# Vectors spread by TensorE and a reordered first batch in an attention and MLP kernel

## The chip, the cores and the metric

One core of a Trainium2 chip. The metric is device microseconds of one execution; a kernel is run several times, and medians are quoted with the lowest and highest run. The profile is one more execution, taken by the hardware profiler, whose span is 1 to 2 us shorter than the timed runs.

## The reference

```python
# q: 8 x 16 x 384 x 64, k and v: 8 x 4 x 384 x 64 (four q heads share a k/v head), all float32
x   = softmax(q @ k.T / 8) @ v          # heads side by side: 8 x 384 x 1024
a1  = alpha1 * x + beta1
tok = einsum('ts,bsd->btd', w_tok, a1)  # the token mix, w_tok 384 x 384
u   = x + lam * tok
a2  = alpha2 * u + beta2
ch  = relu(a2 @ w_ch1) @ w_ch2          # W1 1024 x 4096, W2 4096 x 1024
out = u + lam * ch
```

`alpha1`, `beta1`, `alpha2`, `beta2` and `lam` are vectors of 1024.

## The kernel before

The kernel works through eight batches. A batch has a *side* part (attention, token mix, transposes of `a2`) and a *main* part (`h` = a2 @ W1, `ch` = h @ W2). While TensorE does the main part of one batch, units of the next batch's side part are dropped between its matmuls. Only the side part of the first batch has nothing to hide behind: that is the **prologue**, which ends at the first `h` matmul. I call "main stage" the stretch from there to the first `h` matmul of the second batch.

What the vectors are for: on chip the kernel needs alpha1·lam (`g1`), beta1·lam (`h1`), `lam` and `alpha2` (`al2`) repeated on all 128 partitions, and gets them by broadcast loads, each of which reads the same row of HBM once for every partition (512 KB a vector, as 128 + 384 KB or in one load on the page):

```python
    def bcast(eng, t, ap, lo, hi):
        src = bass.AP(tensor=ap.tensor, offset=ap.offset + lo, ap=[[0, P], [1, hi - lo]])
        eng.dma_start(out=t[:, lo:hi], in_=src)
    # ... cut ...
            t = sb.tile([P, NST, P], f32, tag="tmp", name="a1f", bufs=4)
            nc.vector.tensor_tensor(out=t, in0=x[:, :, cols(p)], in1=bc(g1, p), op=MUL)
            a1s[p] = sb.tile([P, NST, P], bf, tag="a1", name="a1", bufs=2)
            eng = nc.gpsimd if first and p < NP - 2 else nc.vector
            eng.tensor_tensor(out=a1s[p], in0=t, in1=bc(h1, p), op=ADD)
    # ... cut: the prologue's loads ...
        load_k(0)
        nc.scalar.dma_start(out=qst, in_=q[0, :G]...)     # q of heads 0 to 3
        load_q(0, [0], G)                                 # q of heads 4 to 15, GpSimd, casts to bf16
        make_identity(nc, ident)
        load_q(0, [1, 2], G)
        nc.sync.dma_start(out=vst, in_=v[0]...)
        nc.gpsimd.tensor_copy(out=vt[0][:, :, :, :D], in_=vst...)
        place_k(0, 0)
        # ... cut ...
        load_k(1)
        for t, ap in ((g1, moe_alpha1), (lam_t, moe_lam), (h1, moe_beta1)):
            bcast(nc.scalar, t, ap, 0, 256)
            bcast(nc.sync, t, ap, 256, DM)
        bcast(nc.sync, al2, moe_alpha2, 0, DM)
        # ... cut: w_tok, then five tiles of W1; W2 and batch 1's q and v during the units of side(0)
```

A column block `p` is two heads, 128 columns of x. The 18 EXPs of a batch are its softmax tiles. In the prologue the transposes of `a2` of blocks 0 to 4 are DMA transposes, and those of blocks 5 to 7 go through TensorE. In the changed kernel the first batch keeps much of its scratch in `hT`, which nothing else needs yet; so `hT` in its views can be EXP's output, the vector rows, `a` or `a2`.

The softmax here doesn't subtract the row's maximum and nothing guards it: scores larger than these inputs give would overflow.

Of the kernel before, what the change touches and what calls it, by code (L numbers as in the profile page):

```python
# [12 lines left out]
def kernel(  # L13
# [56 lines left out]
    g1, h1, lam_t, al2 = (const.tile([P, DM], f32, tag=n, name=n) for n in ("g1", "h1", "lam", "al2"))  # L70
# [12 lines left out]
    def load_k(b):  # L83
        ks[b] = []
        for h in range(0, Hkv, 2):
            t = sb.tile([P, 2, NST, D], f32, tag="kst", name="kst", bufs=2)
            nc.sync.dma_start(out=t, in_=k[b, h:h + 2].rearrange("h (p st) d -> p h st d", st=NST))
            ks[b].append(t)

    def place_k(b, i):  # L90
        if i == 0:
            k2s[b] = sb.tile([P, NST, Hkv, 2, D], bf, tag="k2", name="k2", bufs=1)
        copies = (nc.vector.tensor_copy, nc.vector.tensor_copy if i else nc.scalar.copy) if b < 2 else [nc.gpsimd.tensor_copy] * 2
        for a in range(2):
            copies[a](out=k2s[b][:, :, 2 * i:2 * i + 2, a, :], in_=ks[b][i].rearrange("p h st d -> p st h d"))
# [5 lines left out]
    def load_q(b, sts=range(NST), i=0):  # L101
        if b not in qrs:
            qrs[b] = sb.tile([P, NST, Hq, D], bf, tag="q_raw", name="q_raw", bufs=1)
        for st in sts:
            nc.gpsimd.dma_start(out=qrs[b][:, st, i:], in_=by_st(q[b])[:, st, i:])
# [8 lines left out]

    def bcast(eng, t, ap, lo, hi):
        src = bass.AP(tensor=ap.tensor, offset=ap.offset + lo, ap=[[0, P], [1, hi - lo]])
        eng.dma_start(out=t[:, lo:hi], in_=src)
# [16 lines left out]
    def tp_ps(shape):  # L134
        return psum.tile(shape, bf, tag="tp", name="tp", bufs=1)
# [6 lines left out]
    def side(b):  # L142
        vb = vt[b % 2]
        x = sb.tile([P, NST, DM], f32, tag="x", name="x", bufs=2)
        xs[b] = x
# [11 lines left out]
        def k_transpose(h0):  # L157
            k2 = k2s[b]
            ps = tp_ps([P, 2 * NST, P])
            for i in range(2 * NST):  # L160
                src = k2[:, i % NST, h0 + i // NST].rearrange("p a d -> p (a d)")
                nc.tensor.matmul(out=ps[:, i, :], lhsT=src, rhs=ident, is_transpose=True,
                                 start=(i == 0), stop=(i == 2 * NST - 1), skip_group_check=True)
            nc.vector.tensor_copy(out=kT[:, :, h0:h0 + 2, :].rearrange("p st h s -> p h st s"),
                                  in_=ps.rearrange("p (h st) s -> p h st s", h=2))

        def q_transpose(g):
            ps = tp_ps([P, 2 * NST, P])
            for i in range(2 * NST):
                h = g * G + 2 * (i // NST)  # L170
                nc.tensor.matmul(out=ps[:, i, :],  # L171
                                 lhsT=qrs[b][:, i % NST, h:h + 2, :].rearrange("p h d -> p (h d)"),
                                 rhs=ident, is_transpose=True, start=(i == 0),
                                 stop=(i == 2 * NST - 1), skip_group_check=True)
            nc.vector.tensor_copy(out=qT[:, :, 2 * g:2 * g + 2, :].rearrange("p st a s -> p a st s"),  # L175
                                  in_=ps.rearrange("p (a st) s -> p a st s", a=2))
# [3 lines left out]
        def scores(i, later=False):  # L180
# [11 lines left out]
            def exp():  # L192
                e = sb.tile([P, 2, 4, P], bf, tag="es", name="es", bufs=EB)
                nc.scalar.activation(out=e, in_=sc, func=EXP, scale=scale_qk)  # L194
                ess[i] = e
# [10 lines left out]
        def av_piece(p, hh):  # L206
# [12 lines left out]
            if hh == 0:  # L219
                if first and p in (0, 2):  # L220
                    r = slice(0, 256) if p == 0 else slice(256, DM)
                    nc.vector.tensor_tensor(out=g1[:, r], in0=g1[:, r], in1=lam_t[:, r], op=MUL)
                    nc.vector.tensor_tensor(out=h1[:, r], in0=h1[:, r], in1=lam_t[:, r], op=MUL)
                return
            rinv = sb.tile([P, 2, NST, 1], f32, tag="rinv", name="rinv", bufs=1)
            nc.vector.reciprocal(out=rinv, in_=av[:, :, :, D:])  # L226
            for hh in range(2):
                c0 = (2 * p + hh) * D
                nc.vector.tensor_tensor(out=x[:, :, c0:c0 + D], in0=av[:, hh, :, :D],  # L229
                                        in1=rinv[:, hh].to_broadcast([P, NST, D]), op=MUL)  # L230
            t = sb.tile([P, NST, P], f32, tag="tmp", name="a1f", bufs=4)
            nc.vector.tensor_tensor(out=t, in0=x[:, :, cols(p)], in1=bc(g1, p), op=MUL)  # L232
            a1s[p] = sb.tile([P, NST, P], bf, tag="a1", name="a1", bufs=2)
            eng = nc.gpsimd if first and p < NP - 2 else nc.vector
            eng.tensor_tensor(out=a1s[p], in0=t, in1=bc(h1, p), op=ADD)  # L235

        def tok(p):
            ps = psum.tile([P, NST, P], f32, tag="av" if first else "sc", name="tok",
                           bufs=1 if first else 2)
            for tt in range(NST):  # L240
                for st in range(NST):
                    nc.tensor.matmul(out=ps[:, tt, :], lhsT=wtokT[:, st, tt * P:(tt + 1) * P],  # L242
                                     rhs=a1s[p][:, st, :], start=(st == 0), stop=(st == NST - 1))
            u = x[:, :, cols(p)]
            nc.vector.tensor_tensor(out=u, in0=ps, in1=u, op=ADD)  # L245
            a2s[p] = sb.tile([P, NST, P], bf, tag="a2", name="a2", bufs=3)
# [15 lines left out]
        def wtok_transpose():  # L262
            wv = wtok_in.rearrange("p tt (s st) -> p tt st s", st=NST)
            for st in range(NST):
                ps = tp_ps([P, NST, P])
                for tt in range(NST):
                    nc.tensor.matmul(out=ps[:, tt, :], lhsT=wv[:, tt, st, :], rhs=ident,
                                     is_transpose=True, start=(tt == 0),
                                     stop=(tt == NST - 1), skip_group_check=True)
                nc.vector.tensor_copy(out=wtokT[:, st, :], in_=ps.rearrange("p a b -> p (a b)"))  # L270
# [10 lines left out]
        if not first:  # L281
            if pe_flip:
# [3 lines left out]
                add(q_transpose, 1)  # L286
            for j in range(NP + 4):
# [3 lines left out]
                if j <= NP:  # L291
                    add(scores2, j)
                    if pe_flip and j in (1, 3):
                        add(q_transpose, 2 + j // 2)
# [8 lines left out]
        add(q_transpose, 0)  # L303
        for i in range(18):
            add(scores, i)
            if i == 1:
                add(q_transpose, 1)
            if i in (5, 9):
                add(q_transpose, i // 4 + 1)
            if i == 4:  # L310
                add(k_transpose, 2)
            if i == 6:
                add(wtok_transpose)
            for p in range(NP):
# [4 lines left out]
                if i == last + 2 and p > 1:  # L319
                    add(tok_flip, p - 2)  # L320
        add(tok, NP - 3)
        add(av_piece, NP - 1, 0)
        add(av_piece, NP - 1, 1)
        add(tok, NP - 2)
        add(a2_transpose, NP - 3)
        add(tok, NP - 1)
        add(a2_transpose, NP - 2)
        add(a2_transpose, NP - 1)
        return us
# [51 lines left out]
    with tc.manual_schedule(engines=order):  # L381

        nc.vector.memset(wtokT, 0.0)
        warm = psum.tile([P, 512], f32, tag="mm", name="warm", bufs=2)
        for _ in range(9):
            nc.tensor.matmul(out=warm[:, :S], lhsT=wtokT[:, 0, :P], rhs=wtokT[:, 1, :],
                             start=True, stop=True)
        load_k(0)
        stage = sb.tile([P, NST, DM], f32, tag="x", name="stage", bufs=2)
        qst = stage[:, 0, :G * NST * D].rearrange("p (h st d) -> p h st d", h=G, st=NST)  # L390
        nc.scalar.dma_start(out=qst, in_=q[0, :G].rearrange("h (p st) d -> p h st d", st=NST))
        load_q(0, [0], G)
        make_identity(nc, ident)
        for t in vt:
            nc.vector.memset(t[:, :, :, D:], 1.0)
        load_q(0, [1, 2], G)
        vst = stage[:, 2, :Hkv * NST * D].rearrange("p (h st d) -> p h st d", h=Hkv, st=NST)
        nc.sync.dma_start(out=vst, in_=v[0].rearrange("h (p st) d -> p h st d", st=NST))
        nc.gpsimd.tensor_copy(out=vt[0][:, :, :, :D], in_=vst.rearrange("p h st d -> p st h d"))
# [3 lines left out]
        load_k(1)  # L403
        for t, ap in ((g1, moe_alpha1), (lam_t, moe_lam), (h1, moe_beta1)):
            bcast(nc.scalar, t, ap, 0, 256)
            bcast(nc.sync, t, ap, 256, DM)
        bcast(nc.sync, al2, moe_alpha2, 0, DM)
        wtok_in = stage[:, 1, :NST * S // 2].bitcast(bf).rearrange("p (tt s) -> p tt s", tt=NST)
        nc.gpsimd.dma_start(out=wtok_in, in_=moe_w_tok.rearrange("(p tt) s -> p tt s", tt=NST))
        be2 = stage[:, 0, DM - NDT:]  # L410
        with nc.allow_non_contiguous_dma(reason="one small vector, once"):
            nc.sync.dma_start(out=be2, in_=moe_beta2.rearrange("(dt di) -> di dt", di=P))
        for c in range(RING):
            load_w1(c)
        loads = {7: [(load_w2, 0, 0, 2)], 25: [(load_q, 1, [0]), (load_q, 1, [1])],
                 31: [(load_q, 1, [2]), (load_v, 1, [0])], 37: [(load_v, 1, [1])], 43: [(load_v, 1, [2])]}
        for i, f in enumerate(side(0)):
# [3 lines left out]
            if i == 4:  # L421
                place_k(0, 1)
# [61 lines left out]
```

## Time and profile before

| | before |
|---|---|
| time, median of 4 (lowest to highest) | 829.96 us (829.51 to 830.88) |
| span of the profile | 828.8 us |
| prologue: start to first `h` matmul | 52.04 us |
| main stage of batch 0: to batch 1's first `h` matmul at 156.08 | 104.04 us |
| the rest | 672.7 us |

The windows view (columns: the stretch; its length, then busy us of PE, PEld, DVE, ACT, POOL, each with its count; the granted TensorE clock; DMA share; GB/s):

```profile
0.00:52.04 52.04, 29.91 (x352) 19.93 (x353) 31.49 (x73) 21.09 (x23) 22.37 (x29) 0.74 1.49 201
52.04:156.08 104.04, 103.02 (x792) 57.75 (x798) 49.72 (x123) 30.80 (x44) 34.30 (x43) 0.98 1.31 183
```

In the prologue no engine is busy for more than 31.5 of 52 us: it is a chain of waits. In the main stage PE is busy for 103.0 of 104.0 us.

### The profile page before, as it was taken

How to read it: one execution, taken by the hardware profiler on the slowest of the kernel's cores; microseconds unless marked ns; L12 is line 12 of the kernel's file. 1: busy time of each engine (PE TensorE's matmuls, PEld its weight loads, DVE VectorE, ACT ScalarE, POOL GpSimd, SP SyncE). 2: the span in 40 equal slices, each digit the busy share in tenths (PEclk: the TensorE clock that was granted, in tenths of full speed). 3: DMA queues.
4: the chain of work that ended last, by engine and by line, in shares of the span. 5: the costliest groups of instructions: out<-in, count | busy, mean ns of one | idle time of the engine just before them, and what ended most of it. 6: DMA issues, size and time to landing. Idle time of an engine off the chain costs nothing.

```text
span 828.8 us, 13904 instructions
## 1 busy us (share of the span) xinstructions
PE 797.1 (96%) x5958; PEld 445.9 (54%) x6011; DVE 350.9 (42%) x728; ACT 219.0 (26%) x287; POOL 187.6 (23%) x229
## 2 busy tenths in 40 slices
PE   5679999999999999999999999999999999999997
PEld 2456555566455654556555664556545565556543
DVE  3854645234452445434443344434444344442222
ACT  3514331233103321043211332133310342102100
POOL 5414441033302250022400224012410221003000
PEclk7869999999999999999999999999999999999999
DMA  9999999799948999499917999379995999119701
GB/s 193 230 145 181 200 210 190 138 175 151 140 97 134 176 169 90 97 166 173 169 46 138 181 169 138 82 128 179 174 91 111 130 176 141 37 55 182 97 38 39
DMA packets 265342, 115.09 MB, mean 139 GB/s; under 512 B 113728, under 2 KB 258496, under 8 KB 265280
## 3 DMA queue, kind: packets, MB, share of 16 engines
q0 software_dynamic: 200832, 83.28, 91.2%
q1 hardware_dynamic: 63488, 30.13, 15.6%
q10 hardware_dynamic: 960, 0.79, 0.4%
q8 instruction: 47, 0.77, 0.4%
q14 instruction: 15, 0.12, 0.0%
HBM read 172.56 MB, written 12.58 MB: 223 GB/s over the span
## 4 chain that ended last, share of the span: by engine, by line
PE 92%; DMA 3%; DVE 2%; issue 1%; ACT 1%; POOL 0%; SPq 0%; DVEq 0%; POOLq 0%
PE h L344 41%; PE ch L368 40%; PE av L217 4%; PE sc L188 4%; PE tok L242 4%; DMA q_raw<-in_q_dram 1%; DMA h<-in_moe_beta_dram 1%; DMA a2T<-a 1%; DVE a L247 1%; ACT hT L352 0%; DVE x L229 0%; DVE x L245 0%; DVE a1f L232 0%; PE tp L171 0%; PE tp L257 0%
## 5 line engine op out<-in xcount | busy, mean ns | idle before, releaser
L344 PE MATMUL h<-a2T,w 128*128 128x384 bf16 (+1 forms) x2048 | 356.6, 327 | 1.2 <-DVE bias L350 0.2
L368 PE MATMUL ch<-w,hT 128*128 128x512 bf16 x1483 | 345.1, 379 | 3.5 <-issue 1.1
L344 PEld LDWEIGHTS <-w 128*128 128x128 bf16 x2048 | 192.9, 98 | 129.4 <-issue 10.6
L127 POOL DMA_DIRECT2D w<-in_moe_w_ch_dram x128 | 112.3, 879 | 549.3 <-PE h L344 514.3
L368 PEld LDWEIGHTS <-hT 128*128 128x128 bf16 x1536 | 142.6, 98 | 155.6 <-issue 4.4
L194 ACT ACTIVATE es<-sc 128x1024 bf16<-128x1024 f32 x144 | 141.2, 1021 | 302.9 <-PE sc L188 302.9
L354 DVE TENSOR_SCALAR hT<-h,bias 128x384 bf16<-128x384 f32 x128 | 78.9, 617 | 186.1 <-PE h L344 185.5
L352 ACT ACTIVATE hT<-h,bias 128x384 bf16<-128x384 f32 x128 | 74.3, 581 | 229.6 <-PE h L344 202.6
L373 DVE TENSOR_TENSOR o<-ch,lam 128x512 f32<-128x512 f32 x48 | 33.0, 688 | 96.9 <-PE ch L368 96.9
L245 DVE TENSOR_TENSOR x<-tok,x 128x384 f32<-128x384 f32 x64 | 35.5, 555 | 82.9 <-PE tok L242 82.9
L217 PEld LDWEIGHTS <-es 128*128 128x128 bf16 x1152 | 52.4, 99 | 23.1 <-issue 1.6
L217 PE MATMUL av<-v,es 128*128 128x65 bf16 x1152 | 56.8, 196 | 0.8 <-ACT es L194 0.6
L242 PE MATMUL tok<-a,wtokT 128*128 128x128 bf16 x576 | 45.0, 226 | 8.8 <-DVE x L245 8.7
L242 PEld LDWEIGHTS <-wtokT 128*128 128x128 bf16 x576 | 38.9, 101 | 22.8 <-issue 6.5
L188 PE MATMUL sc<-qT,kT 64*128 64x384 bf16 (+2 forms) x576 | 46.5, 278 | 0.7 <-DVE qT L175 0.7
L229 DVE TENSOR_TENSOR x<-av,rinv 128x192 f32<-128x192 f32 x128 | 39.8, 352 | 2.3
L247 DVE TENSOR_TENSOR a<-x,al 128x384 bf16<-128x384 f32 x64 | 38.2, 597 | 3.2 <-DMA a2T<-a 1.0
L226 DVE RECIPROCAL rinv<-av 128x6 f32<-128x6 f32 x64 | 12.3, 192 | 59.5 <-PE av L217 59.3
L232 DVE TENSOR_TENSOR a1f<-x,g 128x384 f32<-128x384 f32 x64 | 36.0, 563 | 2.4
L188 PEld LDWEIGHTS <-kT 64*128 64x128 bf16 x576 | 20.1, 95 | 28.0 <-issue 23.6
L374 DVE TENSOR_TENSOR o<-o,x 128x512 f32<-128x512 f32 x48 | 33.2, 692 | 1.6
L235 DVE TENSOR_TENSOR a<-a1f,h 128x384 bf16<-128x384 f32 x58 | 32.5, 561 | 2.2
(38 smaller groups left out, 127.9 us busy)
## 6 DMA issues: line engine op xcount, KB each, us to landing
w<-in_moe_w_ch_dram POOLq DMA_DIRECT2D x135, 512.0 KB, 7.6
out_dram<-o SPq DMA_DIRECT2D x48, 256.0 KB, 2.2
q_raw<-in_q_dram POOLq DMA_DIRECT2D x21, 256.0 KB, 8.8
kst<-in_k_dram SPq DMA_DIRECT2D x16, 192.0 KB, 2.8
w<-in_moe_w_ch_dram POOLq DMA_DIRECT2D x10, 256.0 KB, 12.1
w<-in_moe_w_ch_dram POOLq DMA_DIRECT2D x1, 2048.0 KB, 35.0
v<-in_v_dram POOLq DMA_DIRECT2D x21, 64.0 KB, 8.8
a2T<-a SPq DMA_TRANSPOSE x53, 3.3
```

Source lines behind the costliest of these rows:

```text
L127: nc.gpsimd.dma_start(out=t, in_=w1src[:, :, c * CW * P:(c + 1) * CW * P])
L188: nc.tensor.matmul(out=sc[:, hh, k % 4:k % 4 + n], lhsT=kT[r, sk, 2 * p // G, :], rhs=qT[r, st:st + n, p, :], start=True, stop=True)
L194: nc.scalar.activation(out=e, in_=sc, func=EXP, scale=scale_qk)
L217: nc.tensor.matmul(out=av[:, hh, sq, :], lhsT=ess[k // 4][:, hh, k % 4, :], rhs=vb[:, sk, hk, :], start=(sk == 0), stop=(sk == NST - 1))
L229: nc.vector.tensor_tensor(out=x[:, :, c0:c0 + D], in0=av[:, hh, :, :D], in1=rinv[:, hh].to_broadcast([P, NST, D]), op=MUL)
L232: nc.vector.tensor_tensor(out=t, in0=x[:, :, cols(p)], in1=bc(g1, p), op=MUL)
L242: nc.tensor.matmul(out=ps[:, tt, :], lhsT=wtokT[:, st, tt * P:(tt + 1) * P], rhs=a1s[p][:, st, :], start=(st == 0), stop=(st == NST - 1))
L247: nc.vector.tensor_tensor(out=a2s[p], in0=u, in1=bc(al2, p), op=MUL)
L344: nc.tensor.matmul(out=ps[:, :n], lhsT=w1[:, dt, j * P:(j + 1) * P], rhs=a2T[:, dt, :n], start=(dt == 0), stop=(dt == NDT - 1))
L352: nc.scalar.activation(out=hT[:, nt, :], in_=ps[:, :S], func=RELU, bias=c1)
L354: nc.vector.tensor_scalar(out=hT[:, nt, :], in0=ps[:, :S], scalar1=c1, scalar2=0.0, op0=ADD, op1=mybir.AluOpType.max)
L368: nc.tensor.matmul(out=ps, lhsT=hT[:, nt, ms * P:(ms + 1) * P], rhs=w2[:, nt, cs], start=(nt == 0), stop=(nt == NNT - 1))
```

## The change

The intent is to shorten the prologue. Each vector comes as a few short rows instead of 512 KB. VectorE splits each row into three bf16 parts whose sum is the float32 value, and TensorE spreads them over 128 partitions with a matmul against a selector of ones and zeros (`spread`). In the first batch beta1·lam is no longer added on VectorE or GpSimd: the token mix gets one more matmul, of the row sums of w_tok (`R`) with the beta rows (`H`), zero-padded to 128 rows. q of batch 0 comes by groups of four heads in its own layout and is rearranged by GpSimd. W1's loads are issued after the first of these GpSimd copies and before the others. `a2` has five slots in place of three, and the end of the prologue has a new order, with the split of `lam` (for the main stage) before the small copy that the first `h` matmul waits for.

The diff, cut to its core:

```diff
+            if first:     # first batch: only the multiply is left
+                nc.vector.tensor_tensor(out=a1s[p], in0=x[:, :, cols(p)], in1=bc(g1, p), op=MUL)
+                return
...
-            eng = nc.gpsimd if first and p < NP - 2 else nc.vector
-            eng.tensor_tensor(out=a1s[p], in0=t, in1=bc(h1, p), op=ADD)
+            nc.vector.tensor_tensor(out=a1s[p], in0=t, in1=bc(h1, p), op=ADD)
... token mix
+                if first:
+                    nc.tensor.matmul(out=ps[:, tt, :], lhsT=R[:, tt * P:(tt + 1) * P],
+                                     rhs=H[:, cols(p)], start=False, stop=True)
...
+        def spread(ps_, vs, tag, eng="ACT"):
+            n = len(ps_)
+            ps = psum.tile([P, 4, P], f32, tag=tag, name="vec", bufs=1)
+            w = vs[1] - vs[0]
+            for i, p in enumerate(ps_):
+                nc.tensor.matmul(out=ps[:, i * w:(i + 1) * w], lhsT=sel[:, p:p + 1].to_broadcast([P, P]),
+                                 rhs=rows_b[:, vs[0] * P:vs[1] * P], start=True, stop=True)
+            evac(eng)(out=vecs[:, vs[0]:vs[1], ...], in_=ps[:, :n * w]...)
... units of batch 1's side part
+            for p in range(0, NP if b == 1 else 0, 2):
+                add(spread, (p, p + 1), (2, 4), "tp")
... end of the prologue
         add(a2_transpose, NP - 2)
         add(a2_transpose, NP - 1)
+        add(split, 3, 4)
... loads of the prologue
-        load_k(0)
+        load_k(0, [0])
+        for i, ap in enumerate((moe_alpha1, moe_alpha2, moe_beta1, moe_lam)):
+            nc.sync.dma_start(out=rows_f[:, i * P:(i + 1) * P],
+                              in_=bass.AP(tensor=ap.tensor, offset=ap.offset, ap=[[0, 3], [P, NP], [1, P]]))
+        nc.sync.dma_start(out=vst, in_=v[0].rearrange("h (p st) d -> p h st d", st=NST))
+        load_k(0, [2])
+        load_q4(1)
         make_identity(nc, ident)
+        nc.gpsimd.dma_start(out=wtok_in, in_=moe_w_tok.rearrange("(p tt) s -> p tt s", tt=NST))
+        load_q4(2)
+        load_q4(3)
...
+        nc.gpsimd.tensor_copy(out=vt[0][:, :, :, :D], in_=vst.rearrange("p h st d -> p st h d"))
+        place_q4(1, nc.gpsimd)
+        for c in range(RING - 1):
             load_w1(c)
+        place_q4(2, nc.gpsimd)
-        loads = {7: [(load_w2, 0, 0, 2)], 25: [(load_q, 1, [0]), (load_q, 1, [1])],
-                 31: [(load_q, 1, [2]), (load_v, 1, [0])], 37: [(load_v, 1, [1])], 43: [(load_v, 1, [2])]}
+        loads = {9: [(load_w1, RING - 1), (load_w2, 0, 0, 2)], 20: [(late_loads,)], 30: [(load_q, 1)], 37: [(load_v, 1)]}
```

## The prediction

> **What bounds the kernel now.** I read the page's slices first, then the chain of waits in order of time, then the timelines of VectorE and GpSimd. The slices say where a change can act at all:
>
> ```profile
> span 828.8 us, 13904 instructions
> PE   5679999999999999999999999999999999999997
> ...
> PEclk7869999999999999999999999999999999999999
> ```
>
> From the third slice of 20.7 us on, TensorE is full at full clock: only TensorE work taken away would shorten that, and the change takes none away there. The change lies in the first batch's attention and token mix, a prologue which no matrix work of another batch covers. Its end is the first `h` matmul, at 52.04 us. The busy sums of that stretch (windows view, 0 to 52.04) are PE 29.91, DVE 31.49, ACT 21.09, POOL 22.37 us: no engine is a bound by itself, so waits are. The chain of waits names them (start, length, what):
>
> ```profile
> 3.98 10.29 DMA q_raw<-in_q_dram
> ...
> 17.61 9.60 DMA h<-in_moe_beta_dram
> ...
> 30.05 1.09 DVE a L247
> ...
> 36.45 1.39 DVE a L247
> 37.84 0.03 DVE rinv L226
> 37.87 8.32 DMA a2T<-a
> ...
> 46.28 0.56 DVE a L247
> ...
> 51.74 0.50 PE tp L257 x3
> 52.24 5.56 PE h L344 x24
> ```
>
> Four things. The q of heads 4 to 15 came late, at 14.27. The broadcast vectors came late: g1 and h1 were not complete until 28.2, and all of VectorE's token-mix work stood behind them. From 29 to 42 VectorE ran without a pause, with its `a` multiply at twice its length. Then a slot of `a` had to wait for a DMA transpose. GpSimd's timeline has what lay beside those long multiplies:
>
> ```profile
> 29.72 1.00 POOL L235 TENSOR_TENSOR a<-a1f,h 128x384 bf16<-128x384 f32 x1 [6.80 <-DVE a1f L232]
> 33.12 0.99 POOL L235 TENSOR_TENSOR a<-a1f,h 128x384 bf16<-128x384 f32 x1 [2.40 <-PE av L217]
> ```
>
> And TensorE's clock is half in much of the prologue (0.50 in the 2 us windows from 8 to 16, 32 to 38 and 42 to 54), so the 24 `h` matmuls above take 5.56 us where the same count later in the chain takes 3.92 to 4.03.
>
> [...]
> 1. [...] `a<-x,al` takes 1.07 to 1.39 us beside GpSimd's add and 0.56 us alone (46.28).
> 2. [...] the idle time from 26.8 to 30.07 is followed by windows at 0.50.
> 3. [...] from 5.5 us on, with q's pieces in the queue, the DMA rate falls from about 360 to 160 GB/s, and w1 with longer pieces runs at about 200.
>
> **The change, part by part.** The work on the time is the walk below: I go through the new instruction order of each engine with the durations of the old trace. Durations used: EXP 0.96 apart; a set of scores 0.33 on TensorE when warm (0.54 cold), an `av` pair 0.65 (1.1), a token mix 0.61 (1.1), six transposes 0.35; VectorE per column block: reciprocal 0.22, two multiplies 0.65, g1 multiply 0.48, token-mix add 0.59, al2 multiply 0.47, all start to start and without GpSimd beside it (from 46.28 to 51.13), so 2.4 us; the 768-wide PSUM copy 0.56 on VectorE, and on ScalarE an estimated 0.80 (from its 384-wide copy at 0.48 and EXP's slope of 0.84 ns an element).
>
> Removed: four broadcasts of 512 KB (2 MB at the 300 GB/s seen at 20 to 27 us is 7 us of all DMA engines); the g1 and h1 multiplies by lam (2.75 us of VectorE); GpSimd's six adds and VectorE's two (with them the contention, about 0.5 us on each of four multiplies); the slot wait of 8.3 us, since `a` has five slots in place of three.
>
> Added: the vectors as 24 short rows, two multiplies and five operations to split them, about 2.9 us of VectorE; `spread`, two 256-column matmuls (0.3) and a ScalarE copy of 512 columns (0.57, same slope), four times in the prologue and four in batch 0's main stage; three more matmuls of 128 columns in each token mix (0.61 becomes 0.82); the row sums (about 1 us of VectorE, once); three q and k copies moved from VectorE to ScalarE.
>
> Moved: q comes in 768-byte pieces, each group of heads its own transfer, then a GpSimd copy; W1 is issued after the first such copy; the last W1 tile and W2 later.
>
> The walk. *Start:* k lands as before, 4.05. Scores need only half of q's first group, so the first EXP starts at 6.65 (was 7.59). EXPs 0 to 3 fit without a wait, to 10.5. The split ends at 9.55, the spread at 9.9. q's second group: I estimate landing at 7 [...], the GpSimd copies of v and q end at 9.3 to 9.8, transposes 10.45, VectorE copy 11.1, so EXP 4 starts at 11.55, against 15.5 for EXP 2 before. *Middle:* the weights of the token mix and the row sums hold VectorE to 14.9, scores 6 stand behind them on TensorE, EXP 6 starts at 14.85. From there ScalarE has 12 EXPs, three spread copies (0.57) and three q/k copies (0.80), 15.6 us: with about 1 us of waits EXP 17 ends at 31.4. VectorE has seven `av` groups (1.35) and eight token mixes (1.06), 17.9 us, with about 2 us of waits for TensorE up to 27. *End:* `av` 7 is done at 32.1; VectorE is behind by then: reciprocal of the last pair at 32.8, its g1 multiply to 34.25, the mixes of blocks 6 and 7 follow one after the other through one PSUM buffer (add to 34.75, mix to 35.6, add to 36.2, multiply to 36.8). The transposes of block 7 end 1 us later, but the moved tail puts the split of lam (five operations, 1.25 us) ahead of the small copy which the first `h` matmul waits for: it starts at 38.3.
>
> So the prologue is 52.0 - 38.3 = 13.7 us shorter. Against it: eight spread matmuls in the full main stage, 8 x 0.13 = +1.0. If the clock is warm at the hand-over, the first 24 `h` matmuls save 5.56 - 3.95 = 1.6; I count half, -0.8. 829.9 - 13.7 + 1.0 - 0.8 = 816.4. My walk leaves out small latencies and GpSimd's copies beside VectorE from 12.7 to 15.3; I add 0.6: **817.0 us**.
>
> **The rivals.**
> (a) *TensorE goes cold.* For: it was cold some 27 of the first 54 us, and padding and spreads add to it. Per block, cold: 2.25 x 0.54 + 1.1 + 1.44 + 0.5 = 4.3 us, more than ScalarE's 2.8 and VectorE's 2.4, so it would be the bound. Against: [...] seven dummy matmuls stand in the early gap. I give it 2 to 5 us: 819 to 822.
> (b) *A transfer takes the place of the removed one.* The 2 KB copies of the beta rows are issued at about 9.6 and the first mix needs them at 15; before, a vector of 128 KB took 6.5 to 7.5 us to land. And the DMA transposes took 7.2 to 8.3 us: block 4's, issued at about 30.5, would land at 38.5, just as `h` starts. 0 to 3 us: up to 820.
> (c) *VectorE and ScalarE wait less than I walked*, as the padding and the spread rows end every wait on a vector. The floor is ScalarE: 18 EXPs, four spreads and three copies, 22 us from 6.65, then about 5.5 us for the tail, so `h` at 34: 812 to 813.
> (d) *All hidden*: the main stage then waits for W1, for q of batch 1 or for W2, which is issued later, and the gain is given back. Against: W1's first four tiles should land by about 21 (2 MB at 200 GB/s from 9.5), and batch 1's q at about 42, some 5 us before its transposes are due. 825 and more; I give it 1 in 20.
>
> **Range and chances.** Walk 816.4, (c) to 812.5, (a) and (b) to 822: the range is **812.5 to 822.5**. Faster by over 2% needs less than 813.3, an `h` start at about 35: between my walk and the floor of (c), so **0.15**. Within 2%: **0.83**. Slower: **0.02**; it would take a stall in the main stage.
>
> **What would show it.** First `h` matmul at 36.5 to 41 us (wrong below 35 or above 43). No wait of VectorE or TensorE for a vector's DMA. EXP 4 at 11 to 13 us. The `a` multiply at 0.56 to 0.6 in all eight. The chain's last 6 us before `h` on VectorE, through add, multiply, split and the small copy, not on a DMA. The clock at 0.9 or more between 20 and 36. From the first `h` to the end 777 to 779 us (777.8 before). A long wait of `h` for a DMA transpose or for W1 would make the prediction wrong, and so would a cold TensorE through the middle.

## The result, and the profile after

| | before | after |
|---|---|---|
| time, median of 4 (lowest to highest) | 829.96 us (829.51 to 830.88) | 823.69 us (823.58 to 825.62) |
| ratio to before (95% interval) | | 0.9929 (0.9911 to 0.9946) |
| prologue | 52.04 us | 42.96 us |
| main stage of batch 0 | 104.04 us | 106.33 us |
| the rest | 672.7 us | 672.7 us |

A ratio here is the mean time of one kernel's fast runs over that of the other's fast runs of the same rounds, so it is not quite the ratio of the medians. The change saves 6.3 us, less than 1% but clear of noise, and the time lies above the predicted range of 812.5 to 822.5. The page of the changed kernel:

```profile
span 822.0 us, 14091 instructions
...
PE   6799999999999999999999999999999999999997
...
PEclk9999999999999999999999999999999999999999
```

The first two slices, which held PE digits 5 and 6 and clock digits 7 and 8, are now 6 and 7 at full clock. The windows view by stage:

```profile
0.00:42.96 42.96, 29.87 (x393) 20.20 (x394) 31.01 (x82) 25.83 (x32) 19.56 (x30) 0.96 1.16 165
42.96:149.29 106.33, 104.51 (x805) 58.48 (x804) 49.91 (x123) 32.49 (x46) 34.42 (x43) 0.98 1.38 191
```

The prologue lost 9.1 us and the main stage gained 2.3. Three differences from the predicted walk carry nearly all of the miss: **the start of the prologue, the hand-over to the main stage, and the main stage itself.**

**The start.** Where the walk expected EXP 4 at 11.55 us, it starts at 16.05. The timeline (start, length, engine, line, operation, tiles, count, idle time of the engine before it and what ended that):

```profile
9.48 0.48 DVE L483 TENSOR_TENSOR hT<-hT 24x128 f32<-24x128 f32 x2 [2.64 <-DMA hT<-in_moe_lam_dram]
11.87 0.83 POOL L497 CAST v<-stage 128x768 bf16<-128x768 f32 x1 [6.83 <-DMA stage<-in_v_dram]
12.65 0.94 POOL L461 COPY q_raw<-qh 128x768 bf16<-128x768 bf16 x1
...
12.96 0.50 PE L298 MATMUL vec<-hT,stage 128*128 128x256 bf16 x2 [3.60 <-DVE hT L490]
...
13.65 0.82 PE L174 MATMUL tp<-ident,q_raw 128*128 128x128 bf16 x6 [0.19 <-POOL q_raw L461]
...
16.05 1.02 ACT L199 ACTIVATE hT<-sc 128x1024 bf16<-128x1024 f32 x1 [1.97 <-PE sc L190]
```

Two waits for transfers stand there: VectorE for the rows of `lam`, until 9.45, and GpSimd for `v`, until 11.8. The q copy is not late for q (its transfer, issued at 1.3 us, took 4.5 us to land); it stands behind the `v` copy on GpSimd. TensorE ran `spread` at 12.96, then q's transposes (13.65), then the scores of EXP 4 (15.40). So two gates, rows and `v`, open almost together. SyncE's queue shows when the two transfers were issued, first in the changed kernel and then in the kernel before:

```profile
3.76 0.70 SPq L447 DMA_DIRECT2D hT<-in_moe_lam_dram  x1
4.50 0.43 SPq L449 DMA_DIRECT2D stage<-in_v_dram  x1
```

```profile
1.76 0.46 SPq L398 DMA_DIRECT2D stage<-in_v_dram  x1
```

The four row transfers cost SyncE 0.70 to 0.94 us of issue each, and `v` comes 2.7 us later than before. By then GpSimd's loads fill the DMA engines (126.3% below). The DMA view of the stretch from 4 to 6 us shows it (queue: packets, MB, share of 16 engines, over 100% where packets overlap; q0 is GpSimd's, q1 is SyncE's), before:

```profile
q1 hardware_dynamic: 759, 0.56, 89.4%
q0 software_dynamic: 151, 0.02, 14.9%
```

and after:

```profile
q0 software_dynamic: 559, 0.33, 126.3%
q1 hardware_dynamic: 43, 0.02, 4.7%
```

In these 2 us SyncE's queue moved 0.56 MB and GpSimd's 0.02 before; after, it is 0.02 and 0.33. `v` needed 7.3 us from issue to landing (5.5 before). The packet records show the first row transfer's 24 packets in three interleaved series, 67 ns from one packet to the next in each; which DMA engines moved them the records do not name. All 96 row packets together took 4.7 us, from about 4.2 to 8.9.

From about 12 to 15.5 us the DMA engines then move 8 GB/s, as W1 is issued only behind the q copy, from 13.54.

**The hand-over.** The prologue's end in the timeline:

```profile
40.89 0.56 DVE L258 TENSOR_TENSOR hT<-x,vecs 128x384 bf16<-128x384 f32 x1
...
42.60 0.21 DVE L490 CAST hT<-hT 24x128 bf16<-24x128 f32 x1
42.74 0.17 DVE L515 CAST a2T<-stage 128x8 bf16<-128x8 f32 x1
...
42.96 0.81 PE L379 MATMUL h<-a2T,w 128*128 128x385 bf16 x4 [1.12 <-DVE a2T L515]
44.17 4.91 PE L379 MATMUL h<-a2T,w 128*128 128x385 bf16 x20 [0.39 <-DMA a2T<-hT]
```

The first `h` matmul waits 1.12 us for the small copy behind the split, as predicted. But the fifth, which needs column block 4, waits again: block 4's DMA transpose, issued from 35.1 to 36.3, is still on its way until 44.17. TensorE is cold on top: the clock is 0.50 from 44 to 46 and 0.70 from 46 to 48 us, and the 24 matmuls end at 49.08, 6.1 us after their start.

**The main stage.** TensorE's waits in it, after (us in total, times, longest):

```profile
PE h L379 <- DVE a2T L515: 1.1, 1, 1.1
PE av L222 <- ACT es L199: 0.8, 1, 0.8
```

The first of these lies before the stage's start. Next come the 0.39 us for the transpose, shown above, and two of 0.3. No wait for W1, W2 or q of batch 1 shows.

### The profile page after: what moved, and what is told of

The parts are those of the page before. It is cut to its first block, busy times and chain, and to the rows that moved or that the text cites. A ratio compares the mean times of both kernels' runs of the same rounds, so it can differ in the third digit from the quotient of the medians.

```text
span 822.0 us, 14091 instructions
## 1 busy us (share of the span) xinstructions
PE 801.6 (98%) x6061; PEld 446.9 (54%) x6061; DVE 350.6 (43%) x738; ACT 225.5 (27%) x298; POOL 184.9 (22%) x230
## 4 chain that ended last, share of the span: by engine, by line
PE 87%; ACT 1%; DVE 0%; issue 0%
PE ch L403 41%; PE h L379 36%; PE av L222 3%; PE sc L190 3%; PE tok L246 3%; ACT hT L387 1%; PE tp L268 0%; DVE o L408 0%; DVE o L409 0%; DVE a1f L237 0%; DVE a L239 0%; DVE bias L385 0%
## 5 line engine op out<-in xcount | busy, mean ns | idle before, releaser
L403 PE MATMUL ch<-w,hT 128*128 128x512 bf16 x1536 | 353.5, 379 | 0.3 <-ACT hT L387 0.3
L199 ACT ACTIVATE es<-sc 128x1024 bf16<-128x1024 f32 x126 | 123.5, 1021 | 286.3 <-PE sc L190 286.3
L408 DVE TENSOR_TENSOR o<-ch,vecs 128x512 f32<-128x512 f32 x48 | 33.0, 688 | 93.9 <-PE ch L403 93.9
L222 PEld LDWEIGHTS <-es 128*128 128x128 bf16 x1008 | 45.9, 97 | 21.4 <-ACT es L199 1.0
L222 PE MATMUL av<-v,es 128*128 128x65 bf16 x1008 | 49.2, 193 | 0.8 <-ACT es L199 0.8
L246 PE MATMUL tok<-a,wtokT 128*128 128x128 bf16 x504 | 37.3, 219 | 0.0
L258 DVE TENSOR_TENSOR a<-x,vecs 128x384 bf16<-128x384 f32 x56 | 31.6, 564 | 1.9
L239 DVE TENSOR_TENSOR a<-a1f,vecs 128x384 bf16<-128x384 f32 x56 | 31.2, 558 | 2.2
L237 DVE TENSOR_TENSOR a1f<-x,vecs 128x384 f32<-128x384 f32 x56 | 31.3, 558 | 2.0
## 6 DMA issues: line engine op xcount, KB each, us to landing
w<-in_moe_w_ch_dram POOLq DMA_DIRECT2D x10, 256.0 KB, 12.4
```

The source lines that it names most:

```text
L199: nc.scalar.activation(out=e, in_=sc, func=EXP, scale=scale_qk)
L222: nc.tensor.matmul(out=av[:, hh, sq, :], lhsT=ess[k // 4][:, hh, k % 4, :], rhs=vb[:, sk, hk, :], start=(sk == 0), stop=(sk == NST - 1))
L246: nc.tensor.matmul(out=ps[:, tt, :], lhsT=wtokT[:, st, tt * P:(tt + 1) * P], rhs=a1s[p][:, st, :], start=(st == 0), stop=(st == NST - 1 an ...
L403: nc.tensor.matmul(out=ps, lhsT=hT[:, nt, ms * P:(ms + 1) * P], rhs=w2[:, nt, cs], start=(nt == 0), stop=(nt == NNT - 1))
```

## The experiments

All but one are edits of the changed kernel; each ratio is to the kernel before in the same rounds, whose medians were 829.9 to 830.5 us. Runs of one kernel differ by up to 2.6 us, so differences between experiments of less than about 1 us decide nothing by themselves; the landmarks in the profiles do. A table at the end of the section collects the numbers.

**Theory A, first:** `v` and the rows are late because GpSimd's loads were ahead of them in the DMA engines; without that, EXP 4 starts at 12 and the time falls by the same 4 us. **Rivals:** only the rows matter, or only `v`; the tail is the larger part; or the main stage gives the gain back.

**e1, GpSimd's loads issued after `v` and the first q copy.**

```diff
         make_identity(nc, ident)
-        nc.gpsimd.dma_start(out=wtok_in, in_=moe_w_tok...)
-        load_q4(2)
-        load_q4(3)
...
         place_q4(1, nc.gpsimd)
+        nc.gpsimd.dma_start(out=wtok_in, in_=moe_w_tok...)
+        load_q4(2)
+        load_q4(3)
```

> Theory Q (queue order): v and the four vector rows came late because they were issued on SP's queue after GpSimd's four large transfers had filled the DMA engines. With w_tok and q's third and fourth groups issued only after the GpSimd copy of q's second group, v should land by 8.5 us (11.8 in the changed kernel), the first multiply of the rows should start by 7.5 (9.48), EXP 4 by 13 (16.05), the first h matmul at 39 to 40.5 (42.96), and the time should be 2.5 to 4 us below the changed kernel's 823.7, at 820 to 821. Rival R (the issue itself: each of the four row transfers takes 0.7 to 0.94 us on SP, and v takes 7.3 us whatever else runs): v stays at 11 to 12, EXP 4 at 16, time 823 to 824.

Measured: 824.43 us (823.76 to 825.69), 0.9938. The timeline:

```profile
8.10 0.91 POOL L494 CAST v<-stage 128x768 bf16<-128x768 f32 x1 [5.04 <-DMA stage<-in_v_dram]
...
12.42 1.02 ACT L199 ACTIVATE hT<-sc 128x1024 bf16<-128x1024 f32 x1 [0.68 <-PE sc L190]
...
14.09 0.82 PE L277 MATMUL tp<-ident,stage 128*128 128x128 bf16 x6 [1.70 <-DMA stage<-in_moe_w_tok_dram]
```

The `v` copy starts 3.8 us earlier, the row multiply 2.7 us earlier (6.81), EXP 4 3.6 us earlier. This shows the queue theory. But w_tok now comes late, TensorE waits 1.7 us for it and goes cold (0.50 from 14 to 20 us), and the first `h` matmul is at 42.26, only 0.7 us earlier.

**e2, only the last two q groups late, w_tok left where it was.**

```diff
         nc.gpsimd.dma_start(out=wtok_in, in_=moe_w_tok...)
-        load_q4(2)
-        load_q4(3)
...
         place_q4(1, nc.gpsimd)
+        load_q4(2)
+        load_q4(3)
```

> As the run before, but w_tok stays where it is and only q's third and fourth groups are issued later. Theory Q expects a part of the effect: v at 9 to 10.5 us, EXP 4 at 13.5 to 15, 1 to 2.5 us below the changed kernel. Rival R expects nothing (v 11.8, EXP 4 at 16).

Measured: 827.09 us (825.65 to 828.21), 0.9963. The `v` copy moved half way (10.28), the row multiply hardly (9.33), and EXP 4 not at all (16.2). The rows alone are enough of a gate. The main stage became 110.7 us: 2.1 us of waits for W1, a wait of 1.2 us for block 4's transpose, and a half clock from 44 to 50 us, in which the first 24 `h` matmuls took 8.1 us (6.1 in the changed kernel).

**e3, `v` issued before the rows on SyncE.**

```diff
+        nc.sync.dma_start(out=vst, in_=v[0]...)
         for i, ap in enumerate((moe_alpha1, moe_alpha2, moe_beta1, moe_lam)):
             nc.sync.dma_start(out=rows_f...)
-        nc.sync.dma_start(out=vst, in_=v[0]...)
```

> v issued on SP ahead of the four vector rows, GpSimd's transfers as in the changed kernel. Both theories expect v early, by 8 us (Q) or 8.6 (R: issue at 1.3 plus 7.3). What it tells apart is which of the two late arrivals was the gate: if the rows (split, then spread, which stands ahead of q's transposes on TensorE), EXP 4 stays at 15.3 to 16.5 and the time within 0.8 us of the changed kernel; if v alone, EXP 4 comes to 12 to 13 and the time falls by 3 us or more.

Measured: 825.39 us (825.04 to 827.11), 0.9952. `v` is copied at 6.31, the rows stay at 9.7 and EXP 4 even comes later, at 18.14: the split, now beside GpSimd's copies (11.40 to 14.30), ends 5.6 us after the row multiply starts (3.4 in the changed kernel). With e2: both gates must move, and the rows hold by themselves.

**e4, the split of `lam` after the small copy.**

```diff
-        add(split, 3, 4)
...
         nc.vector.tensor_copy(out=a2Ts[0][:, :, S:S + 1], in_=be2[:, :, None])
+        split(3, 4)
```

> The split of lam put behind the small copy that the first h matmul waits for. By my tail step the first h matmul starts 1.25 us sooner, at 41.7 (42.96), and the time falls by 1.0 to 1.3 us. Rival: the fifth h matmul waited for the DMA transpose of block 4 until 44.17; this lands when it did, so h starts sooner, waits longer inside, and the time falls by 0 to 0.4 us.

Measured: 825.7 us (823.72 to 826.09), 0.9947.

```profile
43.25 0.82 PE L378 MATMUL h<-a2T,w 128*128 128x385 bf16 x4
45.60 1.84 PE L378 MATMUL h<-a2T,w 128*128 128x385 bf16 x6 [1.53 <-DMA a2T<-hT]
```

Without the wait for the split, the wait for block 4's DMA transpose grows from 0.39 to 1.53 us. This run was already 1.4 us later at EXP 6 (21.46), and its transpose was issued 1.6 us later, so `h` does not start sooner by the clock. Counted from the last `a2` multiply it does: 0.8 us after it, 2.1 in the changed kernel. So the transpose was a second gate right behind the first, and with it there the new order of the tail cost nothing that these two traces show.

**e5, both gates moved without starving w_tok.** A tiny GpSimd copy that needs q's first load holds w_tok back to 4.9 us, behind `v`; q's last groups as in e2.

```diff
-        nc.gpsimd.dma_start(out=wtok_in, in_=moe_w_tok...)
-        load_q4(2)
-        load_q4(3)
...
+        nc.gpsimd.tensor_copy(out=stage[:, 2840:2841], in_=qst[:, 2, 0, :1])
+        nc.gpsimd.dma_start(out=wtok_in, in_=moe_w_tok...)
...
         place_q4(1, nc.gpsimd)
+        load_q4(2)
+        load_q4(3)
```

> The run with w_tok late moved v to 8.10 and the rows to 6.81 as theory Q says, but then w_tok itself was waited for (1.7 us) and TensorE went cold from 13 to 20. Here w_tok is issued at 4.9 us, just behind v, held there by a tiny GpSimd copy that waits for q; q's third and fourth groups stay late. If the start was all that my walk had wrong: v by 8.5, EXP 4 at 12 to 13, EXP 5 at 13.5, EXP 6 by 16.5, first h matmul at 38.5 to 40, and 820 to 821 us. Rival W (the gain is given back in batch 0's main stage, whose DMA engines run at 200 GB/s without a pause): first h as said, but h waits for w1 in the main stage, which grows from 106.3 to 108 us and more, and the time is 822 to 824.

Measured: 824.28 us (823.3 to 825.29), 0.9931. The first `h` matmul is at 40.46 and the 24 matmuls take 4.38 us, warm (the clock is 1.00 from 15 to 54 us): the prologue is 2.5 us shorter and well clocked. The time did not move. TensorE's waits in the main stage say where most of it went:

```profile
PE tp L174 <- DMA q_raw<-in_q_dram: 3.7, 3, 1.6
```

After these waits the clock is 0.50 from 56 to 58 us and 0.70 to 60. Batch 1's first `h` matmul is at 150.81, later than in the changed kernel. This is the rival that I had given 1 in 20.

**e6, no spread of the late vectors.** Its output is wrong, which doesn't matter for the time. `h1` and `lam`, which the main stage uses, are set to 0.5.

```diff
-            for p in range(0, NP if b == 1 else 0, 2):
-                add(spread, (p, p + 1), (2, 4), "tp")
...
+        nc.gpsimd.memset(vecs[:, 2:4], 0.5)
```

> Wrong result on purpose: the four spread units in batch 0's main stage are left out, h1 and lam hold 0.5. The main stage of batch 0 took 104.0 us before and 106.3 in the changed kernel. I counted 1.0 us for the eight matmuls of the spread. If the four units cost only that, the stage takes 105.3 us; if they also shift the other units so that TensorE waits for EXP and for the hT copies (1.4 us of such waits in the trace), it takes 104.0 to 104.5. First h as in the changed kernel, 43; time 821.5 to 822.7.

Measured: 827.36 us (825.27 to 827.74), 0.9967. Four units fewer bring q's transposes forward, into a wait of 5.5 us for q, so the run says nothing of what the spreads cost. I repeated it as e13 with q loaded earlier.

**e7, a tail without the DMA transpose of block 4, and warm.** The split last, block 4 transposed on TensorE, nine dummy matmuls in the gaps.

```diff
-            if not pe_flip or first and p < NP - 3:
+            if not pe_flip or first and p < NP - 4:
...
+        add(a2_transpose, NP - 4)
         add(a2_transpose, NP - 3)
         add(tok, NP - 2)
+        add(warmup, 4)
         add(tok, NP - 1)
         add(a2_transpose, NP - 2)
+        add(warmup, 5)
         add(a2_transpose, NP - 1)
-        add(split, 3, 4)
```

> As the tail run (lam's split behind the small copy), and block 4 turned on TensorE, not by DMA, and nine dummy matmuls in the idle time of the tail. In the tail run h started, did four matmuls and waited 1.5 us for block 4's DMA transpose. If that transpose was the second gate, there is no wait for it here and h runs through; the first 24 h matmuls take 3.95 us if the dummies keep the clock, 5 to 5.6 if not. Together 1.3 + 1.5 = 2.8 us below the changed kernel at best (821), 0 to 0.5 if the idle time has nothing to do with the clock and another transpose takes block 4's place.

Measured: 822.66 us (821.33 to 823.32), 0.9913.

```profile
42.04 4.39 PE L381 MATMUL h<-a2T,w 128*128 128x385 bf16 x24
```

The hand-over is now as predicted: 24 matmuls in one piece and warm (1.00 from 34 to 44 us), ended at 46.43 instead of 49.08. Of these 2.65 us, batch 1's first `h` matmul keeps 0.45 (148.84): 1.7 us became waits for W1. That the dummies kept the clock is not shown: e5 had a warm hand-over without them.

**e8, e5 and e7 together.** No new edit.

> The last two together (w_tok behind v, q's groups late, lam's split last, block 4 on TensorE, dummies). If the gains add up: first h at 37 to 38.5, 24 h matmuls in 4 us, 817 to 818.5 us, which is what I predicted for the change itself. If rival W is right, h waits for w1 and the time stays at 820 or above.

Measured: 823.45 us (822.84 to 824.08), 0.9922. Here the prologue is the predicted one (EXP 4 at 12.37, `h` at 38.62), and then TensorE waits:

```profile
52.28 0.23 PE L174 MATMUL tp<-ident,q_raw 128*128 128x128 bf16 x1 [1.60 <-DMA q_raw<-in_q_dram]
53.85 0.61 PE L174 MATMUL tp<-ident,q_raw 128*128 128x128 bf16 x4 [1.34 <-DMA q_raw<-in_q_dram]
```

The main stage is 111.0 us: q of batch 1 lands 25.4 to 26.5 us after its issue at 25.0 to 27.3, TensorE waits 2.9 us for it and runs at 0.52 of its clock from 54 to 60 us, which costs about as much again (an estimate: 6 us at 0.52 lose 2.9). **With a prologue as short as predicted the time is still 823.5 us.** That leaves **theory B**: a sum of transfers bounds the stretch to batch 1, whatever the prologue does. The rival: only their order is bad, q behind the 2 MB of W2's first half.

**e9 and e10, W2's first half issued behind batch 1's q and v,** on the changed kernel and on e8. ("First half" is half of W2's first column half: 2 of its 8 MB as bf16.)

```diff
-        loads = {9: [(load_w1, RING - 1), (load_w2, 0, 0, 2)], 20: [(late_loads,)], 30: [(load_q, 1)], 37: [(load_v, 1)]}
+        loads = {9: [(load_w1, RING - 1)], 20: [(late_loads,)], 30: [(load_q, 1)], 37: [(load_v, 1), (load_w2, 0, 0, 2)]}
```

> The changed kernel with one thing moved: W2's first half (2 MB, needed by batch 0's second matrix product at about 99 us) is issued behind batch 1's q and v, not ahead of them. Theory W2: batch 1's q lands at 51 to 54 us in every version, as it stands behind W2 in the queue, whatever the prologue does. Here q should land by 40. In the changed kernel itself TensorE did not wait for q (the four spread units delay its transposes past 53), so the time should be within 1 us of 823.7; if it falls by 2 us or more, q's lateness cost something that I do not see.

> The all-together run with W2's first half behind batch 1's q. There h started at 38.6, TensorE then waited 2.9 us for q at 50 to 54 and went cold from 53 to 60, and the main stage took 111.0 us. If q behind W2 is what gave the gain back: no wait for q, h at 38.6, the main stage at 104.5 to 106, and 816.5 to 818.5 us. If the DMA engines' total is the bound (some 200 GB/s without a pause from 16 to 120 us), the wait moves to w1 and the time stays at 821 or above.

Measured: e9 824.28 us (823.94 to 825.6), 0.9936; e10 823.59 us (822.68 to 824.72), 0.9923. q lands in 11.6 to 13.6 us in e9 (22.6 to 24.1 in the changed kernel) and in 14.9 to 16.1 in e10 (25.4 to 26.5 in e8), and nothing waits for it. In e10 two `h` matmuls wait 4.3 us instead, nearly all of it here:

```profile
58.17 1.47 PE L381 MATMUL h<-a2T,w 128*128 128x385 bf16 x4 [3.79 <-DMA w<-in_moe_w_ch_dram]
```

The clock is 0.60 in the 4 us after it. The wait moved from q to W1, and batch 1 begins at 149.0, as in the others.

**e11, the kernel before without its broadcast vectors (wrong).** The loads are dropped, the vectors set to 0.5.

```diff
-        for t, ap in ((g1, moe_alpha1), (lam_t, moe_lam), (h1, moe_beta1)):
-            bcast(nc.scalar, t, ap, 0, 256)
-            bcast(nc.sync, t, ap, 256, DM)
-        bcast(nc.sync, al2, moe_alpha2, 0, DM)
...
+            if i == 1:
+                for t in (g1, h1, lam_t, al2):
+                    nc.vector.memset(t, 0.5)
```

> Wrong result on purpose: the kernel before, with its four vectors set to 0.5 by VectorE while it is idle, and their 2 MB of broadcasts left out; all else as before. It tells what the late vectors alone cost. In the old chain VectorE stood from 23.7 to 27.2 waiting for them, and TensorE's token mix to 30; q's landing at 14.3, GpSimd's adds and the slot wait stay. I expect the first h at 45 to 48 (52.0), and the time 3 to 6 us below the kernel before. If the whole gain of the change comes from these 2 MB, it is at 823 to 824.

Measured: 825.82 us (825.53 to 826.24), 0.9949, 4.2 us by the ratio. `h` starts at 47.02. So some two thirds of what the whole change brought comes with leaving out the four broadcasts alone.

**e12, W2 spread over the first W1 tiles** (on e8: 512 KB of W2 beside each of six W1 tiles).

```diff
-            if b == 0 and 2 <= c < 12:
-                load_w2(*((0, 6 + c, 16) if c < 10 else (1, c - 10, 16)))
+            if b == 0 and c < 12:
+                load_w2(*((0, 2 + c, 8) if c < 6 else (1, c - 6, 16)))
...
-                for i in range(1, 8):
+                for i in range(3, 8):
...  the line of loads, unit 37:
+                 37: [(load_v, 1), (load_w2, 0, 0, 8), (load_w2, 0, 1, 8)]
```

> The all-together run with W2's first column half cut into eight pieces of 512 KB: two behind batch 1's q and v, six at one a w1 tile in the main stage, so that neither q nor w1 stands behind 2 MB. If only the order was wrong: no wait for q, no wait of h for w1 above 0.5 us, h at 38.5, batch 1's first h at 143.5 to 145, 816.5 to 818.5 us. If the DMA engines' sum is the bound, waits for w1 or for W2 add up to 4 us again, batch 1's first h is at 148 to 150, and the time 822 to 824.

Measured: 827.93 us (826.81 to 828.96, 5 runs), 0.9972, with 9.3 us of waits for W1 in eight places. My design was at fault: it asks for 1 MB in the time of one W1 tile. At the 3.0 to 3.5 us that e15 mostly needs for one that is 300 GB/s or more (an estimate), and the DMA view of this run shows about 200 between 60 and 105 us.

**e13, e6 again with e9's order of loads (wrong).**

> Wrong result on purpose, as e6 (no spread units in batch 0's main stage), with W2's first half behind batch 1's q, so that its transposes do not wait. From the end of the 24th h matmul to batch 1's first h the kernel before took 98.3 us, the changed one 100.4. If the matmuls of the spread are all, this is 99.5; if the units also shift the others into waits for EXP and for hT, 98.3. Rival: with the transposes 5 us sooner h waits for w1 as in e10, and the stretch is longer than 101.

Measured: 823.77 us (823.28 to 824.11), 0.9921. From the end of the 24th `h` matmul to batch 1's first: 98.28 us here (51.08 to 149.36), 98.27 in the kernel before (57.81 to 156.08), 100.21 in the changed kernel (49.08 to 149.29). The order of loads is not what did it: e9 has it too, with the spread units, and takes 100.34. So the spread units cost the main stage 1.9 to 2.1 us, where I had 1.0.

**e14 and e15, W2 evenly:** on e8 and on e7, 1 MB of W2 after `v`, then 256 KB beside each of twelve W1 tiles, and its second column half after that.

```diff
-            if b == 0 and 2 <= c < 12:
-                load_w2(*((0, 6 + c, 16) if c < 10 else (1, c - 10, 16)))
+            if b == 0 and c < 12:
+                load_w2(0, 4 + c, 16)
...
-                for i in range(1, 8):
+                for i in range(8):
...  the line of loads: W2 gone from unit 9, and
+                 37: [(load_v, 1), (load_w2, 0, 0, 8), (load_w2, 0, 1, 8)]
```

> The all-together run with W2's first column half as 1 MB behind batch 1's q and v (into the idle time of the DMA engines before the first w1 tile is free) and 256 KB beside each of the twelve next w1 tiles, 145 GB/s asked; the second half all behind tile 12. If order was the fault: waits of h for w1 below 1 us, none for q, batch 1's first h at 143.5 to 145.5, 817 to 819 us. If the sum is the bound: batch 1's first h at 148 or later, 822 or more. A wait of the second product for W2 could come in its place, at 99 or 122 us.

> e7 (tail parts and dummies, start as in the changed kernel) with the same order of W2. h in e7 waited 1.7 us for w1 in four places; without these 820 to 821, batch 1's first h at 147. If e14 is below this by 2.5 us or more, the early start pays once the transfers let it.

Measured: e14 **820.86 us** (820.54 to 821.22), 0.9885; e15 821.35 us (820.67 to 821.87), 0.9890. Both beat both kernels, by less than 2% but clear of noise: the intervals, 0.9869 to 0.9902 and 0.9876 to 0.9905, lie below that of the changed kernel (0.9911 to 0.9946). e15 has `h` at 42.57 and waits for neither W1 nor q. e14 has it 4.9 us earlier, at 37.71, and pays with waits for W1:

```profile
60.67 0.83 PE L381 MATMUL h<-a2T,w 128*128 128x385 bf16 x4 [0.47 <-DMA w<-in_moe_w_ch_dram]
...
64.56 1.48 PE L381 MATMUL h<-a2T,w 128*128 128x385 bf16 x8 [0.77 <-DMA w<-in_moe_w_ch_dram]
```

From 56.77 to 92.23 each W1 tile's first matmul comes 3.9 to 4.0 us after the one before (the next at 68.54), where e15 mostly needs 3.0 to 3.5; seven of these waits show, 3.9 us in all. One W1 tile and one piece of W2 are 512 + 256 KB as written on chip; one such pair per 3.93 us is 200 GB/s (400 GB/s as read, since HBM holds them as float32). The windows view of e14 has the same figure at the end of its lines:

```profile
60.00:80.00 20.00, 17.72 (x155) 10.58 (x153) 9.77 (x29) 7.88 (x11) 8.01 (x10) 1.00 1.38 200
80.00:100.00 20.00, 18.07 (x156) 10.30 (x156) 10.99 (x29) 7.05 (x10) 7.72 (x10) 1.00 1.38 200
```

The changed kernel, e8 and e15 have 200 in both stretches as well. So in e14 the transfers set the pace, and an early `h` gains little more: 4.9 us of it are worth 0.5 us, too little for these runs to tell from nothing.

All runs:

| run | median us | ratio | `h` starts | batch 1's `h` | main stage |
|---|---|---|---|---|---|
| before | 829.96 | 1 | 52.04 | 156.08 | 104.04 |
| after | 823.69 | 0.9929 | 42.96 | 149.29 | 106.33 |
| e1 | 824.43 | 0.9938 | 42.26 | 149.45 | 107.19 |
| e2 | 827.09 | 0.9963 | 43.07 | 153.73 | 110.66 |
| e3 | 825.39 | 0.9952 | 44.62 | 150.59 | 105.97 |
| e4 | 825.70 | 0.9947 | 43.25 | 150.93 | 107.68 |
| e5 | 824.28 | 0.9931 | 40.46 | 150.81 | 110.35 |
| e6 (wrong) | 827.36 | 0.9967 | 41.99 | 153.3 | 111.3 |
| e7 | 822.66 | 0.9913 | 42.04 | 148.84 | 106.80 |
| e8 | 823.45 | 0.9922 | 38.62 | 149.60 | 110.98 |
| e9 | 824.28 | 0.9936 | 42.24 | 149.49 | 107.25 |
| e10 | 823.59 | 0.9923 | 38.41 | 149.01 | 110.60 |
| e11 (wrong) | 825.82 | 0.9949 | 47.02 | 151.47 | 104.45 |
| e12 | 827.93 | 0.9972 | 38.06 | 153.43 | 115.37 |
| e13 (wrong) | 823.77 | 0.9921 | 44.28 | 149.36 | 105.08 |
| e14 | 820.86 | 0.9885 | 37.71 | 146.31 | 108.60 |
| e15 | 821.35 | 0.9890 | 42.57 | 147.10 | 104.53 |

Read the column of batch 1's `h`: from e7 to e10 it stays within 0.8 us while `h` starts anywhere from 38.4 to 42.2.

## Why the prediction was wrong

The predicted 817.0 us was 38.3 us to the first `h` matmul and 778.7 from there. Measured were 42.96 and 823.69 - 42.96 = 780.7. The miss of 6.7 us is 4.7 in the prologue and 2.0 after it.

1. **The removal of the broadcasts: right.** No engine waits for a broadcast any more, all eight `a2` multiplies (the prediction's "`a` multiply") take 0.56 us, the clock is 1.00 from 20 to 36 us, and rival (a), a cold TensorE, did not come before the hand-over, but for 14 to 16 us (0.50). e11 gives the broadcasts 4.2 us. But the sign "no wait of VectorE or TensorE for a vector's DMA" did not hold: VectorE waits 2.64 us for the rows that replaced them.
2. **The start of the walk: this step failed.** "The split ends at 9.55" and "the GpSimd copies of v and q end at 9.3 to 9.8": they end at 12.9 and 13.6. I had worked out one landing, that of q's second group, at 7, an estimate that no trace showed; it landed at about 5.8 and was no gate. For the rows and `v` I had put down only when the work behind them ends. I did not work out when SyncE gets to issue `v` behind four row transfers, nor what is already in the engines then. e1 and e5 moved just that, and EXP 4 came at 12.4 and 13.5. The gate cost 4.5 us at EXP 4 and 5.2 at EXP 6 (20.02 for 14.85).
3. **The middle and the tail of the prologue: right in length.** From EXP 6 to `h` it took 22.9 us, and I had 23.4. (The 17.9 us of VectorE there count eight token mixes, and the tail counts the last two again; with six, 15.8 and the 2 us of waits, the walk's 32.8 comes out to 0.1.) The wait for the split was as predicted. Rival (b), block 4's DMA transpose just as `h` starts, was true as well: 0.39 us after, 1.53 in e4.
4. **The main stage: the mechanism of the spread was right, the size was off.** Eight matmuls at 0.13 were to cost 1.0; they cost 1.9 (e13), as the shifted units also bring a wait of 0.8 for an EXP, which is gone in e13. The transpose adds 0.4, and the 0.8 for a warm hand-over was not got. e7 got it with nine dummy matmuls, e5 without any, so what decides it stays open.
5. **Rival (d) was set far too low, and this is the deeper error.** "Batch 1's q at about 42, some 5 us before its transposes are due": it lands between about 51 and 54.5 (issue from 28.1 to 30.4, 22.6 to 24.1 us to landing), as 2 MB of W2 are ahead of it. The old trace had it: there q of batch 1 took 17.5 to 18.2 us from its issue at 34.1 to 37.3, and landed after 51 too. In the changed kernel itself nothing waits for it, as `h` starts late. Had step 2 held, it would have: e8 has the predicted prologue and takes 823.5 us, for the wait for q and the half clock after it. "The change takes none away there", said of the full slices, hid that the stage's length depends on when it starts: 104.0 us in the kernel before, 111.0 in e8.
6. **What remains of theory B.** That the order of loads is the whole matter is refuted by e9 and e10 (the wait only moved), and in part supported by e14 and e15, where W2's even spread gained 3.1 us (on e8) and 1.9 us (on e7) by the ratios with the same bytes. That the transfers are the bound in e14 is shown by the even spacing of its W1 tiles (3.9 to 4.0 us) at 200 GB/s. That they bound the changed kernel itself is not: it has no such wait. Why e1 to e6 differ from one another by a microsecond or two stays open; it goes in part with the clock at the hand-over (the first 24 `h` matmuls took 4.38 us in e5, at 1.00, and 8.1 in e2, at 0.50 from 44 to 50 us).
7. **A reading of the old trace that does not carry its point.** The prediction sets 160 GB/s with q's pieces against 360 before them. But loads that cast to bf16 are counted as written, half of what they read (a W1 tile is 512 KB on the page and 1 MB as float32), and W1 with longer pieces has only 200. At most the step from 200 to 160 is the pieces'. Nothing in the sum rests on it.

## What to carry to other kernels

Before crediting a shorter prologue, add up the transfers that must land by the next fixed point and divide by the rate that the windows view shows: an earlier start moves no bytes, and its gain can come back as a wait for the next load in line (e8: `h` 4.3 us earlier, 2.9 us of waits for q, and a time 0.2 us below the changed kernel's). When a load is moved, work out the queue: when its engine gets to issue it, and what the other queues have by then put in front (`v`: issued 2.7 us later than before and 7.3 us on the way; 3.5 in e1, with three of GpSimd's loads issued behind it). Where two waits end together, removing one can show nothing (EXP 4 at 16.2 in e2 and 18.14 in e3, for 16.05); move both (12.42 in e1), then look for the third.

## What these runs leave open

- How the queues share the DMA engines. From 4 to 6 us of the changed kernel GpSimd's queue moved 0.33 MB and SyncE's 0.02 MB, and `v` took 7.3 us to land; with GpSimd's loads later (e1) it was being copied 3.6 us after its issue at about 4.5. What sets a queue's share is not shown.
- What the layout of the rows costs. Their 96 packets of 512 bytes took 4.7 us in the changed kernel and 1.7 in e1. No experiment tried another layout of the rows.
- What makes SyncE's issue longer for some transfers: 0.70 to 0.94 us for each one of 24 rows (12 KB), against 0.37 to 0.50 for one of 128 partitions and 192 to 384 KB.
- What sets the rate of the loads that cast float32 to bf16: 200 GB/s as written (400 as read), from 60 to 100 us in the changed kernel.
- How long a DMA transpose takes beside such loads: block 4's was issued from 35.1 to 36.3 us, and a matmul waited for it until 44.17.
- What brings the half clock at the hand-over. From 36 to 44 us of the changed kernel the longest idle time of TensorE was 1.12 us, PE was busy for 1.58 of the last 4.0 us, and the clock was 0.50 from 44 to 46. Yet e5 has the same waits before its `h` (1.1 us the longest), was busy for 1.67 of the 4 us from 37.5 to 41.5, and stayed at 1.00.
